# Loading w1 in nine 128-partition pieces, and a LayerNorm copy moved to VectorE

## The chip, the cores and the metric

The kernel runs on one core of a Trainium2 chip. The metric is the device time of one execution in microseconds. TensorE (PE) multiplies, VectorE (DVE), ScalarE (ACT) and GpSimd (POOL) do the elementwise work, and SyncE (SP) issues most of the transfers (DMAs), which run on 16 DMA engines shared by all issuing queues.

## The reference

A pre-LayerNorm block on `x` of 1 x 2048 x 576 in bf16: a linear attention mixer with 32 heads of 18, and then an MLP with 4608 hidden units. Both are added to their input.

```python
qkv = layernorm(x) @ wqkv                       # q, k, v: 32 heads x 18
phi(t) = concat(softmax(t @ w_phi[h]), softmax(-t @ w_phi[h]))   # 36 features a head
kv = phi(k)^T v;  z = sum over rows of phi(k)
o = phi(q) kv / (phi(q) z + 1e-6)
h = x + o @ wo
y = layernorm(layernorm(h))
out = h + gelu(y @ w1 + b1) @ w2 + b2           # w1: 576 x 4608, w2: 4608 x 576
```

## The kernel before

The 2048 rows are 16 tiles of 128, taken as 8 pairs. The code writes the order of every engine's work by hand (a manual schedule): each call below puts its instructions at the end of its engine's queue, and the semaphores are set by the tile framework. What stands earlier in the code runs earlier on that engine.

First comes everything that all rows are needed for: LayerNorm, transposes, the projection of keys and values, the softmax features, and the sums `kv` in a PSUM accumulator (`sums`, L586). The query features come in between. `table` turns the sums into the matrix `kvm`. Then `combine_mm` (L673) multiplies the first pair's transposed query features (`turn_q(0)`, two DMA transposes issued by SP at L572, from the tile `padded`) with `kvm`; `divide`, a transpose (`turn_o_mm`), `residual_mm` with `wo` (L722), the second LayerNorm (`residual_stats`, `second`, `rescale`) and its transpose (`turn2_mm`, L359) follow. `turn2_ev` (L364) copies that transpose from PSUM into `ln2T`, in two parts: five chunks and four chunks of the 576 columns, 64 columns of each tile's two halves a chunk.

Then the MLP. `up` (L1161) multiplies with w1, ScalarE applies GELU (L1183), `down` (L1205) multiplies with w2. The first block has 256 rows. Other pairs' attention work is put in between the products: `leave(1)`, at the third product of the first `down`, calls `combine_mm` for the second pair, whose query tile `turn_q(1)` transposes.

w1 lies in SBUF in two parts, `w1[0]` and `w1[1]`, each `[128, 9, 1152]`: partitions 0 to 63 hold 64 rows of each of nine chunks `c` for one range of 1152 hidden columns, partitions 64 to 127 the same rows for the range 2304 columns further on. `up` walks 18 pairs of 128-column blocks: pairs 0 to 8 read `w1[0]`, pairs 9 to 17 `w1[1]`, and each pair goes over all nine chunks. The DRAM view is

```python
w1v = B_w1.rearrange("(c k) (two f) -> two k c f", k=64, two=2)
```

`load_w1(q, ...)` (L613) issues a piece. The memory of `w1[0]` is lent to other weights until the query weights are folded. The first part's pieces are issued by SP at places in the hand-written order between L1002 and L1095, around the loads of `wo` (L624), `turn_q(0)` and `load_b2` (L638). `close_keys` frees the key tiles, makes `w1[1]` and the first half of w2 in their place, and issues the second part's pieces, by SP and GpSimd in turn. Behind them SP issues `load_w2` (L619) six times for the first half and twice for the second, then `turn_q(1)`, and the last four of w2.

Of the kernel before, what the change touches and what calls it, by code (L numbers as in the profile page):

```python
# [18 lines left out]
FF = 4608  # L19
# [10 lines left out]
KC = 9  # L30
KH = 64
# [14 lines left out]
def kernel(  # L46
# [13 lines left out]
    nc = tc.nc  # L60
# [62 lines left out]
    w1 = [w1_pool.tile([P, KC, FF // 4], BF16, name="w1_0", tag="w1_0")]  # L123
# [215 lines left out]
    pool, vec, syn, sca = nc.gpsimd, nc.vector, nc.sync, nc.scalar  # L339
# [6 lines left out]
    act, dve, gps = nc.scalar.copy, nc.vector.tensor_copy, nc.gpsimd.tensor_copy  # L346
# [16 lines left out]
    def turned_back(key, dst, part, copy):  # L363
        copy(dst[:, 5 * part : 5 + 4 * part, :], flight[key][part])  # L364
# [118 lines left out]
    def key_exp(p, i):  # L483
        if p not in phik:
            phik[p] = exk_pool.tile([P, 2, PW], BF16, name="phik", tag="exk")
        exponentials("k", phik[p], p, i)

    def query_mm(p, i):
        features("q", wqp, p, i, CROSSED)

    def query_exp(p, i):
        if p not in phiq:
            phiq[p] = take(("phiq", p)).rearrange("p (a f) -> p a f", a=2)
        exponentials("q", phiq[p], p, i)
# [23 lines left out]
    def key_weigh(p, i, a, eng):  # L518
        weigh("k", phik[p], p, i, a, eng)
# [10 lines left out]
    def query_weigh(p, part, a, eng):  # L530
        src = phiq[p][:, a, :].rearrange("p (h f) -> p h f", f=DH)
        rk = rescaled[p][:, a, :]
        n = 2 * WH
        g0 = part * 5
        hs = slice(g0 * n, (g0 + 5) * n)
        eng.tensor_tensor(  # L536
            padded[:, a, g0 * P : (g0 + 5) * P].rearrange("p (g k) -> p g k", k=P)[
                :, :, 0:STEP
            ].rearrange("p g (h f) -> p g h f", f=DH),
            src[:, hs, :].rearrange("p (g h) f -> p g h f", h=n),  # L540
            rk[:, hs].rearrange("p (g h o) -> p g h o", h=n, o=1).to_broadcast([P, 5, n, DH]),
            ALU.mult,
        )
        if part:
            m = 2 * COUNT[-1]
            eng.tensor_tensor(
                padded[:, a, KW * P - m * DH : KW * P].rearrange("p (h f) -> p h f", f=DH),
                src[:, 2 * NH - m :, :],
                rk[:, 2 * NH - m :].rearrange("p (h o) -> p h o", o=1).to_broadcast([P, m, DH]),
                ALU.mult,  # L550
            )
# [26 lines left out]
    def sums(p, a):  # L578
        t = 2 * p + a
        left.remove(t)  # L580
        for w in range(KW):
            n = COUNT[w]
            f0 = min(w * STEP, PW - P)
            b = w // 6
            at = (w - BANKS[b][0]) * WV
            nc.tensor.matmul(  # L586
                acc_kv[:, b, at : at + n * VW],
                phik[p][:, a, f0 : f0 + P],
                vals[:, t, FIRST[w] : FIRST[w] + n, :].rearrange("p h v -> p (h v)"),
                start=False, stop=not left, skip_group_check=True,  # L590
            )
# [15 lines left out]
    w1v = B_w1.rearrange("(c k) (two f) -> two k c f", k=KH, two=2)  # L607
    w2v = B_w2.rearrange("(h m p) f -> h p m f", h=2, p=P)
    w2 = []

    def load_w1(q, n, eng):
        c0, half = n // 2 * 3, n % 2
        eng.dma_start(  # L613
            w1[q][half * KH : (half + 1) * KH, c0 : c0 + 3, :],
            w1v[half, :, c0 : c0 + 3, q * FF // 4 : (q + 1) * FF // 4],
        )

    def load_w2(h, n):
        nc.sync.dma_start(w2[h][:, 3 * n : 3 * n + 3, :], w2v[h, :, 3 * n : 3 * n + 3, :])  # L619
# [22 lines left out]
    def close_keys():  # L642
        kctx.close()
        late = ctx.enter_context(
            tc.tile_pool(name="late", bufs=1, side="left", reuse_waits="tile")
        )
        w1.append(late.tile([P, KC, FF // 4], BF16, name="w1_1", tag="w1_1"))
        w2.append(late.tile([P, NM // 2, D], BF16, name="w2_0", tag="w2_0"))
        for n in range(6):
            load_w1(1, n, (nc.sync, nc.gpsimd)[n % 2])  # L650

    def side_pool(name, bufs):
        return ctx.enter_context(
# [56 lines left out]
    def turn_o_ev(part, copy):  # L710
        turned_back("o", oT[0], part, copy)
# [5 lines left out]
    def residual_mm(p, i, pa):  # L717
        cs = slice(i * HALF, (i + 1) * HALF)
        for c in range(KC):
            for a in range(2):  # L720
                rows = slice(a * KH, (a + 1) * KH)
                nc.tensor.matmul(  # L722
                    pa[a], oT[p % 2][rows, c, :], wo[rows, c, cs],
                    start=(c == 0), stop=(c == KC - 1),
                )
        flight["a", p, i] = pa
# [30 lines left out]
    def rescale(t, half):  # L757
        mv, rs = moved[t]
        normalise(ln2[t % 2][:, :, half, :], chunks(t), mv, rs, 0)
# [4 lines left out]
    def place2(t):  # L764
        return ln2T[:, :, t % 4 * P : (t % 4 + 1) * P]
# [7 lines left out]
    def turn2_ev(t, part, copy):  # L773
        turned_back(("2", t), place2(t), part, copy)

    def double_bank():
        pa = two.tile([P, 2, 512], FP32, name="pa", tag="two")
        return [pa[:, a, 0:HALF] for a in range(2)]

    def gelu_table():  # L780
        nc.scalar.activation(spare[:, :], mhalf[:, :], AF.Gelu_apprx_tanh)
# [217 lines left out]
    sums(2, 1)  # L999
    key_weigh(3, 1, 1, pool)  # L1000
    key_weigh(4, 1, 1, pool)
    load_w1(0, 4, syn)  # L1002
    sums(2, 0)
    key_weigh(4, 0, 0, pool)
    query_mm(5, 0)
# [15 lines left out]
    query_sum(0, 1)  # L1021
    key_exp(6, 0)
    key_exp(7, 0)
    load_w1(0, 1, syn)
    query_mm(4, 1)
    key_mm(6, 1)
    query_exp(4, 1)
    load_w1(0, 5, syn)
    query_weigh(0, 1, 0, pool)
    query_mm(6, 1)  # L1030
    key_sum(6, 0)
    key_sum(7, 0)
    key_weigh(7, 1, 0, pool)
    load_w1(0, 2, syn)
    key_exp(6, 1)
    value_mm(6, 0)
    query_exp(6, 1)
# [50 lines left out]
    query_mm(3, 1)  # L1088
    turn_o_mm()
    turn_o_ev(0, dve)  # L1090
    load_w1(0, 3, syn)
    query_mm(2, 0)
    turn_o_ev(1, dve)
    query_exp(2, 1)
    load_w1(0, 0, syn)  # L1095
    residual_mm(0, 1, double_bank())
    query_exp(3, 1)
    load_b2()
# [10 lines left out]
    query_mm(1, 1)  # L1109
    query_mm(5, 1)  # L1110
    close_keys()
    query_exp(1, 1)
    query_exp(5, 1)
# [8 lines left out]
    turn2_mm(0)  # L1122
    rescale(1, 0)
    rescale(1, 1)
    turn2_ev(0, 1, act)
    turn2_ev(0, 0, dve)
    gelu_table()
    load_w2(0, 0)
    load_w2(0, 1)
# [191 lines left out]
```

## Time and profile before

| what | us |
|---|---|
| median of 3 runs | 389.98 |
| lowest, highest run | 388.52, 390.71 |
| span of the profiled execution | 391.7 |
| TensorE busy in it | 383.0 |
| ScalarE, VectorE, GpSimd busy | 163.2, 166.0, 117.8 |

The runs shown were timed apart from the profiled execution, for which the page gives the span, 391.7 us from the first to the last instruction; nothing of it lies outside that. The profile names a group by line, engine, operation and tiles (`out<-in`); DRAM and SBUF tiles of w1 and w2 both show as `w`, w_phi's as well. `SPq` and `POOLq` are the queues in which SP and GpSimd issue transfers. "issue" in the chain is time in which the engine waited for nothing that the profile shows.

### The profile page before, as it was taken

The page shows a single profiled execution, that of the slowest core. Times are in us where ns is not written, and L with a number is a line of the kernel's source. Part 1 is how long each engine was busy: PE and PEld are TensorE (multiplying, and loading weights), DVE is VectorE, ACT ScalarE, POOL GpSimd, SP SyncE. Part 2 cuts the span into 40 slices and gives each one's busy share as a digit, 9 for nine tenths or more (in the row PEclk, how much of TensorE's full clock was granted, in tenths as well). Part 3 has the DMA queues.
Part 4 walks back from the last instruction along what each step waited for, and adds up shares of the span by engine and source line. Part 5 has one row for each costly group of instructions (what it writes and reads, how often), then busy time and mean ns, then how long its engine had stood idle before and what let it go on. Part 6 is the DMA issues. An engine that isn't in the chain of part 4 may idle for free.

```text
span 391.7 us, 10190 instructions
## 1 busy us (share of the span) xinstructions
PE 383.0 (98%) x4475; PEld 269.0 (69%) x4475; DVE 166.0 (42%) x364; ACT 163.2 (42%) x291; POOL 117.8 (30%) x161
## 2 busy tenths in 40 slices
PE   7999999799999999999999999999999999999997
PEld 3778779479978887844457887444677764447773
DVE  6998997385249388590019322000480000000100
ACT  2998995478500850046650000666300016661000
POOL 6399998116404654144003111000031110000120
PEclk9999999899999999999999999999999999999999
DMA  8977599999455578433003462000071000000000
GB/s 250 259 128 128 93 218 188 238 313 248 148 105 102 98 105 136 94 66 68 2 2 62 89 108 48 17 1 2 2 105 47 17 15 2 2 2 0 17 28 19
DMA packets 74096, 34.93 MB, mean 89 GB/s; under 512 B 61028, under 2 KB 71524, under 8 KB 74052
## 3 DMA queue, kind: packets, MB, share of 16 engines
q1 hardware_dynamic: 72944, 32.78, 40.3%
q0 software_dynamic: 336, 1.33, 1.2%
q8 instruction: 35, 0.57, 0.7%
q10 hardware_dynamic: 772, 0.17, 0.2%
q14 instruction: 9, 0.07, 0.1%
HBM read 16.47 MB, written 2.36 MB: 48 GB/s over the span
## 4 chain that ended last, share of the span: by engine, by line
PE 93%; ACT 2%; DMA 2%; issue 1%; DVE 1%; SPq 0%
PE po L1205 36%; PE ph L1161 36%; PE pk L450 8%; PE pv L450 5%; PE pa L722 4%; DMA w<-in_A_wqkv_dram 2%; PE acc_kv L586 1%; PE pn L673 1%; ACT home L472 1%; ACT shared L412 0%; DVE xh L731 0%; PE pW L419 0%; PE pW L405 0%; PE pT L359 0%; PE pX L377 0%
## 5 line engine op out<-in xcount | busy, mean ns | idle before, releaser
L1183 ACT ACTIVATE home<-ph,b1col 128x512 bf16<-128x512 f32 (+1 forms) x180 | 98.4, 598 | 169.1 <-PE ph L1161 165.9
L1205 PE MATMUL po<-w,home 128*128 128x288 bf16 (+2 forms) x1152 | 143.3, 286 | 0.0
L1161 PE MATMUL ph<-shared,w 64*128 64x512 bf16 (+2 forms) x1638 | 141.3, 331 | 0.6 <-ACT shared L364 0.6
L1205 PEld LDWEIGHTS <-home 128*128 128x128 bf16 x1152 | 109.4, 98 | 32.1 <-issue 1.8
L1161 PEld LDWEIGHTS <-w 64*128 64x128 bf16 x1638 | 80.3, 94 | 60.5 <-issue 0.7
L1209 DVE TENSOR_TENSOR ot<-po,hb 128x288 bf16<-128x288 f32 (+2 forms) x32 | 14.4, 453 | 106.4 <-PE po L1205 96.7
L450 PEld LDWEIGHTS <-home 64*128 64x128 bf16 x864 | 42.9, 95 | 13.6 <-issue 3.3
L1194 POOL TENSOR_TENSOR hb<-xh,b2bc 128x576 f32<-128x576 bf16 x16 | 20.4, 1273 | 104.6 <-DVE ot L1209 102.8
L536 POOL TENSOR_TENSOR padded<-home,rq 128x540 bf16<-128x540 bf16 x32 | 34.9, 1102 | 34.5 <-DVE rq L528 18.9
L731 DVE TENSOR_TENSOR xh<-pa,xh 128x288 bf16<-128x288 f32 x32 | 13.0, 447 | 72.4 <-PE pa L722 72.4
L274 POOL TENSOR_TENSOR rs<-va,mhalf 128x1 f32<-128x1 f32 x16 | 8.8, 549 | 110.9 <-DVE va L272 110.9
L507 POOL TENSOR_TENSOR phik<-phik,rk 128x576 bf16<-128x576 bf16 x28 | 33.4, 1218 | 1.4 <-DVE rk L503 1.2
L472 ACT ACTIVATE home<-pk 128x576 bf16<-128x576 f32 x32 | 18.6, 665 | 12.7 <-PE pk L450 10.4
L450 PE MATMUL pk<-wqp,home 64*128 64x288 bf16 x288 | 20.5, 293 | 2.8 <-issue 2.8
L501 DVE TENSOR_REDUCE sk<-phik 128x64 f32<-128x1152 bf16 x16 | 21.0, 1312 | 1.7 <-ACT phik L472 1.6
L527 DVE TENSOR_REDUCE sk<-home 128x64 f32<-128x1152 bf16 x16 | 21.0, 1310 | 0.0
L686 DVE RECIPROCAL rec<-pn 128x18 f32<-128x18 f32 (+1 forms) x32 | 8.0, 249 | 28.5 <-PE pn L673 28.5
L450 PE MATMUL pv<-wv,home 64*128 64x288 bf16 x288 | 19.6, 283 | 0.0
L472 ACT ACTIVATE phik<-pk 128x576 bf16<-128x576 f32 x32 | 18.7, 656 | 1.8 <-PE pk L450 1.1
L450 PE MATMUL pk<-shared,home 64*128 64x288 bf16 x288 | 19.3, 283 | 0.0
L722 PE MATMUL pa<-wo,shared 64*128 64x288 bf16 x288 | 18.6, 283 | 0.0
L722 PEld LDWEIGHTS <-shared 64*128 64x128 bf16 x288 | 13.9, 94 | 4.5 <-issue 0.5
(76 smaller groups left out, 208.3 us busy)
## 6 DMA issues: line engine op xcount, KB each, us to landing
w<-in_B_w_dram SPq DMA_DIRECT2D x21, 432.0 KB, 8.7
out_dram<-ot SPq DMA_DIRECT2D x15, 144.0 KB, 2.2
xh<-in_A_x_dram SPq DMA_DIRECT2D x3, 576.0 KB, 6.8
wo<-in_A_wo_dram SPq DMA_DIRECT2D x4, 324.0 KB, 8.0
w<-in_B_w_dram POOLq DMA_DIRECT2D x3, 432.0 KB, 13.0
wv<-in_A_wqkv_dram SPq DMA_DIRECT2D x2, 576.0 KB, 8.7
w<-in_A_wqkv_dram SPq DMA_DIRECT2D x1, 576.0 KB, 6.0
wqp<-wqp SPq DMA_DIRECT2D x2, 288.0 KB, 3.9
```

The costliest lines, as they stand in the source:

```text
L450: nc.tensor.matmul(dst[:, a, 0:HALF], lhs[rows, c, :], w[rows, slot, i * HALF : (i + 1) * HALF], start=(n == 0), stop=(n == KC - 1),)
L472: nc.scalar.activation(rows[:, :, i * HH : (i + 1) * HH, s, :], flight[key, p, i][:, :, 0:HALF].rearrange("p a (h f) -> p a h f", f=DH), A ...
L501: nc.vector.tensor_reduce(sk[:, :, :], part_of(dst, i), AX.X, ALU.add)
L507: eng.tensor_tensor(part, part, flight["r" + key, p, i][:, a, :].rearrange("p (h o) -> p h o", o=1).to_broadcast([P, NH, DH]), ALU.mult,)
L527: nc.vector.tensor_reduce(sk[:, :, :], part_of(phiq[p], i), AX.X, ALU.add)
L536: eng.tensor_tensor(padded[:, a, g0 * P : (g0 + 5) * P].rearrange("p (g k) -> p g k", k=P)[:, :, 0:STEP].rearrange("p g (h f) -> p g h f", ...
L722: nc.tensor.matmul(pa[a], oT[p % 2][rows, c, :], wo[rows, c, cs], start=(c == 0), stop=(c == KC - 1),)
L1161: nc.tensor.matmul(ph[half][:, lo:hi], w1[p_ // 9][rows, c, p_ % 9 * P : (p_ % 9 + 1) * P], ln2T[rows, c, base + lo : base + hi], start=(c ...
L1183: nc.scalar.activation(hidden(m), ph[half][:, 0:width], AF.Gelu_apprx_tanh, bias=b1col[:, m : m + 1], scale=1.0,)
L1194: nc.gpsimd.tensor_tensor(hb[:, :], xh[:, t, :], b2bc[:, :], ALU.add)
L1205: nc.tensor.matmul(po[:, :], hidden(m)[:, i_ * P : (i_ + 1) * P], w2[m // 18][:, m % 18, cs], start=(j == 0), stop=(j == NM - 1),)
L1209: nc.vector.tensor_tensor(ot[:, cs], po[:, :], hb[:, cs], ALU.add)
```

## The change

Each part of w1 is loaded in nine pieces, one for each chunk `c`, with 128 partitions and 1152 columns (288 KB), where it was six pieces of three chunks on 64 partitions (432 KB). The SBUF side of a piece is `[128, 1152]`, the DRAM side `[2, 64, 1152]`. The first part's nine loads take the six places of the order, in rising `c`; the bytes issued ahead of `wo` and `turn_q(0)` stay the same (four pieces of 432 KB before, six of 288 KB after). Of the second part SP issues five pieces and GpSimd four, where it was three each. The second copy of the first tile's transpose, `turn2_ev(0, 1, ...)`, moves from ScalarE to VectorE, behind the first copy.

```diff
-    def load_w1(q, n, eng):
-        c0, half = n // 2 * 3, n % 2
+    def load_w1(q, c, eng):
         eng.dma_start(
-            w1[q][half * KH : (half + 1) * KH, c0 : c0 + 3, :],
-            w1v[half, :, c0 : c0 + 3, q * FF // 4 : (q + 1) * FF // 4],
+            w1[q][:, c, :],
+            w1v[:, :, c, q * FF // 4 : (q + 1) * FF // 4],
         )
...
-        for n in range(6):
-            load_w1(1, n, (nc.sync, nc.gpsimd)[n % 2])
+        for c in range(KC):
+            load_w1(1, c, (nc.sync, nc.gpsimd)[c % 2])
...
-    load_w1(0, 4, syn)
+    load_w1(0, 0, syn)
+    load_w1(0, 1, syn)
...
-    load_w1(0, 1, syn)
+    load_w1(0, 2, syn)
...
-    load_w1(0, 5, syn)
+    load_w1(0, 3, syn)
+    load_w1(0, 4, syn)
...
-    load_w1(0, 2, syn)
+    load_w1(0, 5, syn)
...
-    load_w1(0, 3, syn)
+    load_w1(0, 6, syn)
+    load_w1(0, 7, syn)
...
-    load_w1(0, 0, syn)
+    load_w1(0, 8, syn)
...
-    turn2_ev(0, 1, act)
     turn2_ev(0, 0, dve)
+    turn2_ev(0, 1, dve)
     gelu_table()
```

## The prediction

> **What bounds the kernel now.** I read the page first (the chain, the queues and the list of DMA issues), then the chain in order of time, then the DMA queue's own timeline, then windows over the stage in which w1 is loaded.
>
> ```profile
> span 391.7 us, 10190 instructions
> PE 93%; ACT 2%; DMA 2%; issue 1%; DVE 1%; SPq 0%
> q10 hardware_dynamic: 772, 0.17, 0.2%
> xh<-in_A_x_dram ACTq DMA_DIRECT2D x1, 144.0 KB
> w<-in_A_w_phi_dram ACTq DMA_DIRECT2D x2, 9.0 KB, 3.5
> w<-in_A_w_phi_dram ACTq DMA_DIRECT2D x1, 2.5 KB
> out_dram<-ot SPq DMA_DIRECT2D x1, 16.0 KB, 1.4
> ```
>
> TensorE carries 93% of the chain: what delays it is paid in full, and it has no slack later to win anything back. So the question is which of its waits the change shortens or makes. From the chain in order of time (start, duration, what):
>
> ```profile
> 68.17 0.73 PE pn L673 x22
> 68.90 1.70 PE pk L450 x26
> 70.60 2.77 issue
> 73.37 0.86 PE pk L450 x10
> 85.48 0.48 ACT shared L364
> 86.00 17.88 PE ph L1161 x342
> 103.89 0.35 PE po L1205 x2
> 104.24 0.62 PE pn L673 x22
> 104.86 7.85 PE po L1205 x64
> ```
>
> At 68.17 TensorE multiplies with the first transposed query tile (L673), at 86.00 the MLP begins, at 104.24 the second query tile is needed. Two holes stand ahead of the MLP: 2.77 us at 70.60, which no instruction explains, and the ScalarE copy at 85.48. No step of the chain waits for w1. How the transfers stand in SP's queue, and w1's share of GpSimd's:
>
> ```profile
> 46.53 2.63 SPq L613 DMA_DIRECT2D w<-in_B_w_dram  x4
> 49.20 1.26 SPq L624 DMA_DIRECT2D wo<-in_A_wo_dram  x2
> 55.84 6.72 SPq L572 DMA_TRANSPOSE shared<-padded  x2
> 62.61 0.84 SPq L624 DMA_DIRECT2D wo<-in_A_wo_dram  x1
> 63.51 1.30 SPq L613 DMA_DIRECT2D w<-in_B_w_dram  x2
> 64.85 0.61 SPq L638 DMA_DIRECT2D b2bc<-in_B_b_dram  x1
> 67.03 1.93 SPq L613 DMA_DIRECT2D w<-in_B_w_dram  x3
> 69.08 16.87 SPq L619 DMA_DIRECT2D w<-in_B_w_dram  x8
> 91.78 3.13 SPq L572 DMA_TRANSPOSE phit<-padded  x2
> 94.97 4.85 SPq L619 DMA_DIRECT2D w<-in_B_w_dram  x4
> 67.65 2.08 POOL L613 DMA_DIRECT2D w<-in_B_w_dram  x3 [1.63 <-PE acc_kv L586]
> ```
>
> Four of the six pieces of w1's first part go out at 46.53, ahead of wo and of the transposes that the step at 68.17 reads. The reader should keep this order: the changed pieces stand in the same places. The next fence has busy time by engine in stretches (the last three columns are the TensorE clock, the DMA engines' busy share, GB/s), and one row of the DMA issues between 46 and 100 us:
>
> ```profile
> 6.00:9.00 3.00, 2.08 (x29) 1.53 (x26) 2.33 (x9) 0.87 (x1) 2.57 (x8) 1.00 1.03 378
> 50.00:56.00 6.00, 6.00 (x102) 4.78 (x98) 5.30 (x7) 5.52 (x12) 5.59 (x7) 1.00 1.07 215
> 67.00:73.40 6.40, 3.63 (x68) 2.60 (x67) 3.63 (x12) 2.39 (x4) 2.07 (x3) 1.00 1.06 212
> 73.40:77.00 3.60, 3.60 (x35) 2.42 (x37) 0.82 (x2) 1.19 (x2) 0.00 (x0) 0.58 1.05 250
> 86.00:90.00 4.00, 4.00 (x92) 4.00 (x93) 3.93 (x6) 3.85 (x8) 1.74 (x2) 1.00 1.07 355
> wo<-in_A_wo_dram SPq DMA_DIRECT2D x3, 324.0 KB, 11.4
> ```
>
> With 64-partition pieces in flight (50 to 56, 67 to 73.4) all 16 engines are busy, yet move 212 to 215 GB/s; with 128-partition loads (6 to 9, 86 to 90) they move 355 to 378. A wo load of 324 KB takes 11.4 us to land: 0.33 MB at 215 GB/s is 1.5 us, so it waited behind the w1 pieces issued before it (four of 0.44 MB, 1.77 MB, 8.2 us). Transfers of SP's queue are served in the order of issue.
>
> The Trainium skill ("SBUF — State Buffer", section "Door 1: The DMA port swizzle") says that DMA bandwidth depends on how many of SBUF's 16 ports the partitions reach, and that 64 partitions in a row reach 8. The trace agrees: 212 against 355. By that rule the change helps.
>
> **The change, part by part.**
>
> *How a new piece is split over the engines.* This decides the case, and the trace has no piece of the new shape. What it has is the ACT queue, with a query up to 3.43 us, when its first load is over:
>
> ```profile
> q10 hardware_dynamic: 144, 0.15, 14.2%
> ```
>
> The first load has 128 rows and shows 144 packets: 128 and one closing packet from each of 16 engines. The page has 772 in all, so 628 belong to the three w_phi loads, of 128x2, 128x2 and 72 rows of 36 bytes (9.0, 9.0 and 2.5 KB): 584 rows and 44 closing packets, which is 16 + 16 + 12. Seventy-two rows went to 12 engines, the largest number up to 16 that divides 72; dealt out as evenly as can be, 15 would have shared them. A transfer is thus cut into equal parts along its outermost dimension. The old piece has 64 rows outermost on both sides, so 16 engines. The new piece has 128 partitions outermost in SBUF, but the DRAM side is `w1v[:, :, c, ...]`, whose outermost dimension is the 2 of `two`, with 64 rows inside; the two steps (half a row, a whole row) cannot be merged into one of 128. Equal parts of both sides: 2 engines. The ends are 2 and 16; I take 2, since the nearest row (72 on 12) shows division and not filling up. Both ends are priced below.
>
> The Trainium skill ("DMA: Bandwidth & Descriptors", section "Why a DMA increments its semaphore by 16 and not by 1") states this: the number of engines is the largest up to 16 that divides the slowest dimension of both patterns. By that rule it is two, and on SP's queue always the same two; the row of 72 agrees, and no run here shows a slowest dimension of 2.
>
> *Price of a piece.* An engine at full rate moves 378 / 16 = 23.6 GB/s (6 to 9 us). Two take 0.295 MB in 6.24 us. The slow end is 212 / 16 = 13.3 GB/s, 11.1 us; I take 6.24, because the two parts write to the two halves of the partitions and nothing shares a port with them. So w1's first part costs 9 x 6.24 = 56 us on these two engines. In the second part SP issues 5 pieces (31 us); GpSimd's 4 go through its own queue, and I take them on other engines (a rival otherwise).
>
> *The queue of the two engines, step by step.* SP issues at 46.53; the first data flows 1.4 us later (my estimate from the page's 1.4 us for the shortest transfer), 47.9.
> - Six pieces (c = 0 to 5, all now ahead of wo): 37.4, to 85.3.
> - Two wo loads, each 0.33 MB / 378 GB/s = 0.9: to 87.1. The two transposes of the first query tile, 3.1 by their issue row at 91.78: to 90.2, landed (1.4) at 91.6. L673, at 68.17 before, starts 23.4 later; TensorE is in order, so all behind it waits, and with it ScalarE (the remaining exponentials) and VectorE (the divisions and LayerNorm), which have nothing else to do there.
> - From L673 to the MLP were 17.8 us. The hole of 2.77 falls in a pause and goes, and the copy's 0.5 (below): the MLP could begin at 91.6 + 14.5 = 106.1. But the third wo load (0.9) and pieces 6 to 8 (18.7) end at 109.8, landed 111.2. The first products need all nine chunks: start 111.2.
> - Nine of the 18 pairs of columns use the first part: 17.88 / 2 = 8.9, to 120.1. The tenth needs the second part: b2 (0.4) and five pieces (31.2) end at 141.4, landed 142.8: a wait of 22.7. The other nine pairs end at 151.7, or 153.2 with the clock at 0.58 for 3.6 us (row 73.40:77.00) after the pause, 1.5.
> - Behind these stand eight loads of w2 (0.44 MB / 378 = 1.17 each, 9.4) to 150.8 and the two transposes of the second query tile (3.1) to 153.9, landed 155.3. L673's second use, at 104.24 before, starts 51.1 later. The last four w2 loads (4.7) land at 160.0; the first down product uses the last of them 4.2 after L673's start (0.62 for L673, then 29 products of 7.85 / 64 = 0.123), at 159.5: 0.5 more.
>
> Sum: 51.1 + 0.5 = 52 us (rounded). Nothing after 104 depends on these engines in a new way, so it is neither won back nor grows.
>
> *More issues.*
>
> ```profile
> L613 SPq DMA_DIRECT2D w<-in_B_w_dram x9: 602/619/646, 46.5 to 68.3; - x9
> ```
>
> Each piece costs SP 0.62 us. Three more in the first part: two ahead of the wo loads, covered by SP's wait for `padded` until 55.84; without that cover 1.2 us. One more after it and two more in the second part, 1.9, go ahead of w2, whose place is set by the two engines. GpSimd issues one more, 0.62, idle until 82.07 (its next work is the second LayerNorm's). Costed at nothing, between 0 and 1.9.
>
> *The copy.*
>
> ```profile
> 84.61 0.48 DVE L364 COPY shared<-pT 128x640 bf16<-128x640 bf16 x1
> 85.33 0.62 ACT L364 COPY shared<-pT 128x512 bf16<-128x512 bf16 x1
> PE ph L1161 <- ACT shared L364: 0.6, 1, 0.6
> ```
>
> The ScalarE copy waits for the last exponential and holds TensorE 0.6. On VectorE it follows the first copy at 85.09 and takes 0.4 (four chunks against five in 0.48): ready at 85.5 against 85.95, a gain of 0.5. VectorE's next two copies wait for TensorE until 85.46, so they lose nothing; ScalarE reaches its table load sooner. Here it is hidden behind the wait for w1.
>
> Forecast: 390 + 52 = 442 us. The sum is made in an execution whose span is 391.7, 1.7 above the median 389.98; I add the difference to the median.
>
> **Rivals.**
>
> *The pieces use all 16 engines (the other side).* For it: the 128 partitions on the SBUF side, and 355 GB/s where loads fill them. Against: the 12 engines of the 72 rows. Then w1's 5.3 MB take 15 us instead of 25 and land earlier, but nothing on the chain waits for them; only the copy's 0.5 is left: 389.5. If the hole at 70.60 (2.77, and 1.5 of slow clock behind it) came from the crowded engines and goes, 385. It decides from about five engines on: six pieces, 1.77 MB, must be through between 47.9 and about 63 for the transposes to land by 68, 117 GB/s, five times 23.6.
>
> *GpSimd's pieces fall on the same two engines.* Nothing in the trace excludes it. Each that does adds 6.2 to the queue ahead of the second part's end: 448 for one, 467 for all four.
>
> *The two engines run at the contended rate.* 14 pieces x 4.9 more = 68 us: 510. Against: no neighbour on their ports.
>
> *The transposes are not held up.* If they go past the w1 pieces, L673 is on time, but the second part still lands at about 140; the sum stays within 4 us of the forecast. So no case of its own.
>
> **How the numbers follow.** Two engines 0.86: alone 0.52 (442), with one GpSimd piece 0.24 (448), all four 0.05 (467), at the contended rate 0.03, something milder between 395 and 426 0.02. Sixteen engines 0.14: 389.5 0.08, 385 0.06. About 0.5% (2 us) is what a measurement can tell from no change. One row of the DMA share by slices, from 3 to 9 us in 40 slices, gives the lower bound:
>
> ```profile
> GB/s 399 446 392 415 372 390 211 110 199 254 128 95 179 170 230 300 284 323 284 330 369 384 392 438 346 438 376 338 330 330 422 392 361 369 369 369 461 369 338 369
> ```
>
> Its fastest slice, 461, is 28.8 GB/s an engine, 5.1 us a piece, 14 x 1.1 = 16 less. Range: from there, 426, up to 460 (one GpSimd piece, and pieces at 355 GB/s / 16, 14 x 0.4, and further slow-clock stretches of 1.5 each); the first two cases lie in it, 0.76, and part of the third.
>
> **What will show it.** Few engines: a DMA busy share near 2/16 and under 60 GB/s from about 55 to 85; w1 issues with a landing of tens of us; L673 waiting for the transposes about 20 us; L1161 waiting for w1 at its tenth pair, about 20 us; the remaining stages as long as before. Sixteen engines would show 350 GB/s at 50 and 67 us, and L1161 at about 85.5. The forecast is wrong if w1's landings stay under 15 us.

## The result, and the profile after

| | before | after |
|---|---|---|
| median, us | 389.56 (388.52 to 390.71) | 453.26 (453.1 to 453.87) |
| span of the profiled execution, us | 391.7 | 451.3 |
| mean granted TensorE clock in it | 0.995 | 0.932 |

The change makes the kernel slower by a factor of 1.163 (95% interval 1.160 to 1.166), 63.7 us. Forecast were 442 us and a range of 426 to 460. The lines of the page that answer to those of before (the chain by engine, the first product with w1, the product with the first query tile, and GpSimd's own DMA queue, q0):

```profile
span 451.3 us, 10197 instructions
PE 75%; SPq 13%; DMA 8%; ACT 1%; DVE 1%; issue 1%; POOL 0%
L1163 PE MATMUL ph<-shared,w 64*128 64x512 bf16 (+2 forms) x1638 | 148.0, 342 | 22.3 <-DMA w<-in_B_w_dram 22.3
L672 PE MATMUL pn<-kvm,shared 128*128 128x57 bf16 (+1 forms) x22 | 1.2, 229 | 31.0 <-DMA shared<-padded 31.0
q0 software_dynamic: 2112, 1.19, 1.0%
```

TensorE's share of the chain fell from 93% to 75%. What took its place is SP's queue, an engine that computes nothing, and transfers. Two waits of TensorE make 53.3 us: 31.0 before it may use the first transposed query tile, 22.3 for w1. (Line numbers moved by one or two: L672 was L673, L1163 was L1161, L1207 was L1205.) SP's queue shows how it came about:

```profile
45.58 24.32 SPq L612 DMA_DIRECT2D w<-in_B_w_dram  x6
69.94 14.55 SPq L623 DMA_DIRECT2D wo<-in_A_wo_dram  x2
84.61 11.54 SPq L572 DMA_TRANSPOSE shared<-padded  x2
96.20 0.58 SPq L623 DMA_DIRECT2D wo<-in_A_wo_dram  x1
96.84 6.07 SPq L612 DMA_DIRECT2D w<-in_B_w_dram  x3
102.96 3.57 SPq L637 DMA_DIRECT2D b2bc<-in_B_b_dram  x1
106.72 26.02 SPq L612 DMA_DIRECT2D w<-in_B_w_dram  x5
132.85 18.82 SPq L618 DMA_DIRECT2D w<-in_B_w_dram  x8
152.19 7.20 SPq L572 DMA_TRANSPOSE phit<-padded  x2
```

Before, four issues of w1 took 2.63 us; now six take 24.32. Single issues take up to 6.83 us, where they took 0.62: SP cannot even hand over a piece before an earlier one has moved, and everything behind it in the order waits: the wo loads are issued at 69.94 instead of 49.20, the transposes at 84.61 instead of 55.84. The windows say why (the last two columns are the DMA engines' busy share and GB/s), and so does the count of packets from 50 to 56 us:

```profile
6.00:9.00 3.00, 2.65 (x37) 2.06 (x34) 2.90 (x10) 1.21 (x2) 2.58 (x7) 1.00 1.05 394
48.00:66.00 18.00, 18.00 (x353) 14.80 (x350) 15.18 (x17) 13.64 (x25) 16.62 (x15) 1.00 0.14 51
DMA packets 136, 0.31 MB, mean 51 GB/s; under 512 B 2, under 2 KB 2, under 8 KB 136
```

For 18 us the 16 engines are busy 0.14 of the time, about 2 of 16, and move 51 GB/s, 25.5 for each of two; at full load one moves 394 / 16 = 24.6. In 6 us about one piece passes, and it shows two short closing packets, where the load of 128 rows in the prediction, on 16 engines, shows 16. The other engines stand idle, and the queue still crawls.

### The profile page after: what moved, and what is told of

The parts are those of the page before. It is cut to its first block, busy times and chain, and to the rows that moved or that the text cites. A ratio compares the mean times of both kernels' runs of the same rounds, so it can differ in the third digit from the quotient of the medians.

```text
span 451.3 us, 10197 instructions
## 1 busy us (share of the span) xinstructions
PE 390.7 (87%) x4474; PEld 269.6 (60%) x4475; DVE 166.2 (37%) x365; ACT 162.8 (36%) x290; POOL 119.3 (26%) x162
## 4 chain that ended last, share of the span: by engine, by line
PE 75%; SPq 13%; DMA 8%; ACT 1%; DVE 1%; issue 1%; POOL 0%
PE po L1207 31%; PE ph L1163 27%; PE pk L450 7%; DMA w<-in_B_w_dram 6%; SPq L612 5%; PE pv L450 4%; PE pa L721 4%; SPq L572 3%; SPq L623 3%; DMA shared<-padded 1%; PE pn L672 1%; SPq L618 1%; PE acc_kv L586 0%; ACT shared L412 0%; DVE xh L730 0%
## 5 line engine op out<-in xcount | busy, mean ns | idle before, releaser
L1163 PE MATMUL ph<-shared,w 64*128 64x512 bf16 (+2 forms) x1638 | 148.0, 342 | 22.3 <-DMA w<-in_B_w_dram 22.3
L1207 PE MATMUL po<-w,home 128*128 128x288 bf16 (+2 forms) x1151 | 143.6, 286 | 0.5 <-DMA w<-in_B_w_dram 0.5
L1163 PEld LDWEIGHTS <-w 64*128 64x128 bf16 x1638 | 81.4, 98 | 87.8 <-DMA w<-in_B_w_dram 24.0
L1207 PEld LDWEIGHTS <-home 128*128 128x128 bf16 x1152 | 109.3, 98 | 32.9 <-issue 2.5
L672 PE MATMUL pn<-kvm,shared 128*128 128x57 bf16 (+1 forms) x22 | 1.2, 229 | 31.0 <-DMA shared<-padded 31.0
L672 PEld LDWEIGHTS <-shared 128*128 128x128 bf16 x22 | 1.1, 125 | 31.3 <-DMA shared<-padded 31.3
```

The source lines that it names most:

```text
L1163: nc.tensor.matmul(ph[half][:, lo:hi], w1[p_ // 9][rows, c, p_ % 9 * P : (p_ % 9 + 1) * P], ln2T[rows, c, base + lo : base + hi], start=(c ...
L1207: nc.tensor.matmul(po[:, :], hidden(m)[:, i_ * P : (i_ + 1) * P], w2[m // 18][:, m % 18, cs], start=(j == 0), stop=(j == NM - 1),)
```

## The experiments

Each ratio is to the kernel before.

**1. The copy alone.**

```diff
-    turn2_ev(0, 1, act)
     turn2_ev(0, 0, dve)
+    turn2_ev(0, 1, dve)
```

> Before with one edit: the second copy of the first tile's transpose goes to VectorE, w1 loaded as before. If the copy's step is right (ready 0.5 us sooner, nothing else late), the time is 0.3 to 0.6 us under before. Rival: TensorE's hole at the start of the MLP is w1's (the profile of before also names a w transfer there), and the time is unchanged within 0.2 us.

Measured: ratio 0.9996 (0.9981 to 1.0011). In the trace the step does what was said; the timeline of all engines at the start of the MLP has no wait ahead of the first product:

```profile
81.46 0.98 PE L359 MATMUL pT<-ident,shared 128*128 128x128 bf16 x13
82.51 0.28 PE L1161 MATMUL ph<-shared,w 64*128 64x128 bf16 x3
```

The 0.6 us wait for ScalarE's copy is gone, and nothing took its place. In the time it is not resolved: 0.5 us is 0.13%, inside the interval. So the copy has no part in the 64 us, and its gain is seen in the trace alone.

**2. All 16 engines, everything else as changed.**

```diff
-    w1v = B_w1.rearrange("(c k) (two f) -> two k c f", k=KH, two=2)
+    w1v = B_w1.rearrange("(c k) (two f) -> (k two) c f", k=KH, two=2)
...
-            w1v[:, :, c, q * FF // 4 : (q + 1) * FF // 4],
+            w1v[:, c, q * FF // 4 : (q + 1) * FF // 4],
```

> The changed kernel with one edit: w1's rows are read in another order, so that the DRAM side of a piece is one run of 128 rows with an even step of half a row, instead of 2 times 64. Sizes, number, order and queues of the pieces are the same; the values in w1 are permuted, so the output is not the reference's. Theory (two engines, because the DRAM side begins with a 2): 16 engines take part, 350 GB/s while w1 loads, L672 at about 68 us, time 389 (0.5 under before, or 385 if the 2.77 us hole goes for good). Rival (the smaller pieces, their number, or their order in front of wo cost the time): it stays above 440.

Measured: 388.92 us, ratio 0.9963 (0.9950 to 0.9976). Size, number, order and queue of the pieces are those of the changed kernel; one dimension on the DRAM side makes 64 us. Windows:

```profile
50.00:52.00 2.00, 2.00 (x38) 1.59 (x34) 1.83 (x3) 1.52 (x4) 2.00 (x3) 1.00 0.96 370
67.00:73.40 6.40, 5.89 (x106) 4.43 (x103) 3.91 (x13) 3.80 (x7) 2.39 (x4) 1.00 1.02 339
```

370 and 339 GB/s where before moved 215 and 212: full 128-partition pieces do load faster. The time falls by only 1.4 us, the copy's gain in it, since the kernel before waits for w1 nowhere. This trace has no hole at 70 us.

**3. The same pieces as two halves.** To keep w1's contents, each piece is issued as two of 64 partitions, with 64 rows outermost on both sides.

```diff
-        eng.dma_start(
-            w1[q][:, c, :],
-            w1v[:, :, c, q * FF // 4 : (q + 1) * FF // 4],
-        )
+        for two in range(2):
+            eng.dma_start(
+                w1[q][two * KH : (two + 1) * KH, c, :],
+                w1v[two, :, c, q * FF // 4 : (q + 1) * FF // 4],
+            )
```

> The changed kernel with each of its pieces issued as two, one for the 64 partitions of each half, so that both sides of a transfer have 64 rows outermost: eighteen issues a part, each of 147 KB; order, bytes and contents as in the changed kernel. Theory (a transfer's engines follow from its outermost dimensions): all 16 engines, L672 at 68 to 69; SP needs 0.62 us for each of nine more issues a part, which delays w2 by about 3 us: 389 to 393. Rival (small pieces in this order cost the time): above 420.

Measured: 389.99 us, ratio 0.9996 (0.9970 to 1.0022). Twice as many and smaller pieces, in the changed order, cost nothing. SP's queue:

```profile
45.93 8.07 SPq L613 DMA_DIRECT2D w<-in_B_w_dram  x12
55.45 6.52 SPq L572 DMA_TRANSPOSE shared<-padded  x2
79.47 6.21 SPq L619 DMA_DIRECT2D w<-in_B_w_dram  x8
```

Twelve issues take 8.07 us, 0.67 each, and the transposes go out on time. w2 goes out 10 us later than before, and nothing waits for it. Neither number, size nor order was the cause.

**4 and 5. Eight and four engines.** w1's DRAM side gets the shape 8 times 16 or 4 times 32 rows, in pieces of the same size; the edit shown is the one for four.

```diff
-    w1v = B_w1.rearrange("(c k) (two f) -> two k c f", k=KH, two=2)
+    w1v = B_w1.rearrange("(c k) (two f) -> c (k two) f", k=KH, two=2)
...
-            w1v[:, :, c, q * FF // 4 : (q + 1) * FF // 4],
+            w1v[0:4, c % 4 * 32 : (c % 4 + 1) * 32, q * FF // 4 : (q + 1) * FF // 4],
```

> The changed kernel with w1's DRAM side given the shape 8 times 16 rows (a step of 64 rows outside, half a row inside); same bytes and pieces, other values in w1. Theory (equal parts along the outermost dimension): 8 engines, a piece in 1.5 us, above the five engines from which I worked out that nothing waits: 389 to 391. Rival (any outermost dimension under 128 falls back to two or one engine): 440 or more.

> The same with 4 times 32 rows. Theory: 4 engines, a piece in 2.95 us; six pieces, wo and the transposes end at 70, landed 71 to 74 instead of before 68: L672 3 to 6 us late, the rest of w1 in time, the second query tile 3 to 6 us late: 393 to 398. Rival: as for 8 times 16, 440 or more; or no cost at all, 389.

Measured: 397.37 us, ratio 1.0170 (1.0142 to 1.0197) with 8; 421.92 us, 1.0791 (1.0765 to 1.0818) with 4. With the two of the changed kernel and the 16 of the second experiment the ladder is 453, 422, 397, 389. The mechanism holds (a window with four engines, from 50 to 55 us, is busy 0.27 and moves 101 GB/s: 25 an engine again), but both sizes were missed: 8 engines cost 6.7 us, not nothing, and 4 cost 31 instead of 3 to 8. "About five engines are enough" was wrong; with eight the wait lies at the second query tile, 4.3 us in two, and what holds its transposes there was not traced further. With four, L672 waited 23.4 us and the transposes stood in SP's queue for 21.47:

```profile
50.00:55.00 5.00, 5.00 (x86) 3.95 (x84) 4.90 (x6) 4.52 (x9) 4.58 (x6) 1.00 0.27 101
PE pn L672 <- DMA shared<-padded: 23.4, 1, 23.4
61.14 21.47 SPq L572 DMA_TRANSPOSE shared<-padded  x2
```

**6. Four engines without GpSimd's pieces.**

```diff
-            load_w1(1, c, (nc.sync, nc.gpsimd)[c % 2])
+            load_w1(1, c, nc.sync)
```

> The kernel with 4 times 32 rows, with all nine pieces of w1's second part issued by SP, none by GpSimd. That kernel came out at 422 where 393 to 398 was expected, and its transposes took from 67 to 88 us while GpSimd's pieces were moving. Theory (GpSimd's pieces share engines with SP's queue and take turns with it, packet by packet): without them L672 starts at 71 to 74 us instead of 90; the second part, 9 x 2.95 behind the first, lands at 108 and is waited for 11 us, the second query tile comes at 121: about 409. Rival (four engines are slow for transposes by themselves): L672 stays at 90 and the time goes to 422 + 12 = 434.

Measured: 420.7 us, ratio 1.0784 (1.0756 to 1.0811). The same two lines, and the wait for w1:

```profile
PE pn L672 <- DMA shared<-padded: 7.9, 1, 7.9
61.60 10.57 SPq L572 DMA_TRANSPOSE shared<-padded  x2
PE ph L1163 <- DMA w<-in_B_w_dram: 15.8, 5, 4.0
```

L672 waits 15.5 us less (23.4 and 7.9): GpSimd's pieces did hold up the transposes in the four-engine kernel. The whole stays the same because SP's queue has now nine pieces of the second part, and TensorE pays at L1163. My 409 was 12 us short: I had left three pieces of the first part, 3 x 2.95 = 8.9 us, out of the queue ahead of the second part, which was complete at 116.8 instead of 108. The other 3 us were not taken apart.

**7 and 8. Who issues the second part.** In the changed kernel, all nine pieces by GpSimd, or all nine by SP.

```diff
-            load_w1(1, c, (nc.sync, nc.gpsimd)[c % 2])
+            load_w1(1, c, nc.gpsimd)        # seven; nc.sync in eight
```

> The changed kernel with all nine pieces of w1's second part issued by GpSimd, none by SP. Theory (a GpSimd piece too runs on two engines, but on changing pairs): the second part lands by about 95, SP's two engines lose 29 us of work, the wait at the tenth pair is gone; the transposes are as late as in the changed kernel or 6 us later: 420 to 430. Rival (GpSimd's pieces stay on the same two engines as SP's): no better than the changed kernel, 453 or more.

> The changed kernel with all nine pieces of the second part issued by SP. Theory (in the changed kernel one of GpSimd's four pieces runs on SP's two engines while these are busy, and cost 6.4 us between 67 and 80): L672 starts at about 92 instead of 98, and the second part ends 4 x 5.75 - 6.4 = 17 us later: 470. Rival (no such meeting, the 6 us by which L672 came later than forecast have another cause): L672 stays at 98 and the time is 453 + 23 = 476.

Measured: 440.58 us, ratio 1.1280 (1.1252 to 1.1307) by GpSimd; 471.18 us, 1.2061 (1.2042 to 1.2081) by SP. The waits, GpSimd's kernel first, then SP's:

```profile
PE pn L672 <- DMA shared<-padded: 43.9, 1, 43.9
PE ph L1163 <- DMA w<-in_B_w_dram: 4.8, 1, 4.8
```

```profile
PE pn L672 <- DMA shared<-padded: 24.2, 1, 24.2
PE ph L1163 <- DMA w<-in_B_w_dram: 45.5, 9, 6.5
```

With none, four and nine of GpSimd's pieces L672 waits 24.2, 31.0 and 43.9 us. So the meeting of the two queues is shown: four pieces cost the changed kernel 6.8 us ahead of L672, the rival "one GpSimd piece falls on the same two engines" (6.2). The packets of the two queues show the sharing. The first two rows are the changed kernel from 72 to 76 us, the other two the seventh experiment from 74 to 82 (q0 is GpSimd's queue, q1 SP's; packets, MB, share of the 16 engines' time):

```profile
q0 software_dynamic: 171, 0.72, 47.3%
q1 hardware_dynamic: 28, 0.06, 4.2%
q0 software_dynamic: 928, 1.58, 87.4%
q1 hardware_dynamic: 49, 0.10, 9.5%
```

GpSimd's four pieces fill 0.473 x 16 = 7.6 engines, about two each, and SP's queue moves 7 packets a microsecond, where it moved 22 from 66 to 68: a third, so its two engines are among them. All nine by GpSimd removes the wait at the tenth pair, as expected, and fills 14 engines; but it holds up the transposes by 20 us instead of 7, so 440 and not 420 to 430. SP's queue is held to a third for about 10 us (72 to 82) instead of 5 (71 to 76), as if two of the nine pieces lay on its engines. That is not all of the 20, and the rest is open.

**9 and 10. One part in nine pieces, the other in six.**

```diff
-        for c in range(KC):
-            load_w1(1, c, (nc.sync, nc.gpsimd)[c % 2])
+        for n in range(6):
+            load_w1_six(1, n, (nc.sync, nc.gpsimd)[n % 2])    # nine; the first part in ten
```

> The changed kernel with only w1's second part loaded as before, in six pieces. Theory (one queue of two engines, in order): the transposes land at about 92, the first part at about 111; the second part comes soon behind, before its use at 120, so that wait is gone: 26 us over before, 416. Rival (each part costs by its bytes, half of the whole each): 421 here and the two halves add up to the whole 64.

> The changed kernel with only w1's first part loaded as before, in six pieces. Theory: five pieces at 5.8 us start behind 68 us and are through at 98 to 105, used first at 95; the w2 loads and the transposes of the second query tile behind them land at about 115 to 118 instead of 97: 10 to 14 us over before, 400 to 404. With the first part's 26 that is less than the whole 64, because the second part then waits in the queue behind the first. Rival (costs add): 38 us, 428.

Measured: 437.16 us, ratio 1.1204 (1.1172 to 1.1236) with the first part in nine; 413.04 us, 1.0584 (1.0556 to 1.0613) with the second. The excesses are 47 and 23, against forecasts of 26 and 10 to 14. They add to 70, not far above the 64 of both, so this pair does not tell a queue from costs that add: inconclusive on that point. What the traces do show is which wait each part makes: with the first part in nine, TensorE waits 31.7 us for the first query tile and 9.0 for w1; with the second, not at all for that tile and 17.3 for w1, as the steps of the prediction have it. The sizes were short in part because, of transfers that share the engines, I counted those of SP's queue only: in 6 us beside GpSimd's pieces SP's queue moves 34 packets in the ninth (74 to 80 us) and 44 in the tenth (75 to 81), where it moves 126 in 6 us once GpSimd's are through (the tenth, 84 to 90). How much of the missing 21 and 9 us that makes was not worked out.

**11. The first part behind the transposes.** The six early pieces are issued behind the wo loads and the transposes; the lines further up that lose them are left out here.

```diff
     load_wo(2)
+    for c in range(6):
+        load_w1(0, c, syn)
```

> The changed kernel with the first part's six early pieces issued behind the wo loads and the first query tile's transposes instead of ahead of them. Theory (the two engines' total work decides, not who is first): L672 is on time, 31 us of TensorE's longest wait gone, but w1's first part starts 16 us later and lands at 117 to 124, the second part at 146 to 153: 453 to 460, no gain. Rival (the late transposes are the cost): 453 - 31 = 422.

Measured: 462.56 us, ratio 1.1862 (1.1828 to 1.1895). TensorE's longest wait, 31 us, is gone, and the kernel is 9 us slower still, 2.6 us above the 453 to 460 that I expected:

```profile
63.13 48.50 SPq L612 DMA_DIRECT2D w<-in_B_w_dram  x9
PE ph L1159 <- DMA w<-in_B_w_dram: 62.1, 12, 6.1
```

(L1159 is L1163 of the changed kernel.) The same queue is paid at another place, and it started later. The longest wait was not the cost; the total work of two engines was.

**12. Both halves at once, with the contents right.** Before, with the copy on VectorE and the second part's pieces for partitions 64 to 127 issued by ScalarE beside SP's.

```diff
-        for n in range(6):
-            load_w1(1, n, (nc.sync, nc.gpsimd)[n % 2])
+        for n in range(1, 6, 2):
+            load_w1(1, n, nc.scalar)    # behind table(1); SP's three stay in place
```

> Before, with two edits: the copy on VectorE, and of w1's second part the three pieces of partitions 64 to 127 issued by ScalarE's queue at 67 us beside SP's three pieces of partitions 0 to 63 (GpSimd issues none), so that both halves are written at once. If the halves' ports are what held the load at 212 GB/s, the rate from 67 to 73 is 300 or more and the hole at 70 us closes: 388.5 to 389. Rival (the rate is set by something else in 64-partition pieces): 212 GB/s as before and 390.

Measured: 389.44 us, ratio 0.9983 (0.9962 to 1.0004), not told apart from before. In the stretch that I had named the rate did not rise, but later it did. The rows are two windows, and for the second of them the packets of SP's queue (q1) and ScalarE's (q10):

```profile
67.00:73.40 6.40, 6.07 (x105) 4.36 (x105) 4.45 (x14) 3.59 (x7) 0.00 (x0) 1.00 1.05 210
75.00:79.00 4.00, 4.00 (x70) 3.20 (x66) 3.56 (x13) 1.92 (x4) 0.79 (x2) 1.00 1.06 351
q1 hardware_dynamic: 323, 0.71, 52.9%
q10 hardware_dynamic: 327, 0.68, 51.2%
```

The 210 GB/s, like before's 212, are SP's queue alone: ScalarE issues from 67.19 us on, but its first packet of w1 moves just before 73. From 75 to 79 both queues carry 64-partition pieces of w1, one for each half, and move 351 GB/s, as much as the 128-partition pieces of the second experiment (339 to 370). So the 300 or more of the theory is reached, at a later time than I had named, and the rival's 212 is not what two queues give: two 64-partition transfers side by side do load at the rate of one of 128. Two queues that write the same half were not tried, so it is not shown whether the halves or the second queue raised the rate. The rule of the Trainium skill that I brought in for the 212 ("SBUF — State Buffer", section "Door 1: The DMA port swizzle": bandwidth by the number of ports reached) agrees with both, 212 for one half and 351 for two. Why the rate is still 221 GB/s from 73 to 75, with both queues moving, is open. The time stays because TensorE waits for w1 nowhere. There is no hole at 70 us in this execution, though the rate there was still 210, so it is not a higher rate that closed it.

## Why the prediction was right, and where its sum was short

The deciding step was right: a piece whose DRAM side begins with a dimension of 2 runs on two engines, read from 772 packets of another queue. The second and third experiments show it from both sides: change that dimension and the 64 us are gone. The Trainium skill ("DMA: Bandwidth & Descriptors", section "Why a DMA increments its semaphore by 16 and not by 1") is borne out for a slowest dimension of 2 by the two closing packets and the 51 GB/s. The steps:

| step | forecast | after |
|---|---|---|
| rate of the two engines, GB/s | 47.2 | 51 |
| L673, now L672, first use | 91.6 | 98.15 |
| w1's first part complete at TensorE | 111.2 | 118.4 |
| w1's second part complete | 142.8 | 149.7 |
| second query tile used (in the last column its second half) | 155.3 | 162.97 |

The rows of the last column are in the chain and in TensorE's timeline (the bracket has the wait ahead):

```profile
98.15 1.21 PE L672 MATMUL pn<-kvm,shared 128*128 128x57 bf16 x22 [30.98 <-DMA shared<-padded]
118.41 6.84 PE L1163 MATMUL ph<-shared,w 64*128 64x128 bf16 x80 [4.19 <-DMA w<-in_B_w_dram]
162.97 0.48 PE L672 MATMUL pn<-kvm,phit 128*128 128x57 bf16 x11 [1.88 <-DMA phit<-padded]
115.47 5.70 SPq L612
127.00 22.69 DMA w<-in_B_w_dram
```

- *GpSimd's pieces.* I had them on other engines in the likeliest case and kept the meeting as a rival at 0.24. It is what happened: all rows from L672 on are 6.5 to 7.7 us late, and without GpSimd's pieces L672 waits 6.8 us less and starts at 92.45, against the 91.6 of the forecast. The 448 for that rival is nearer than my 442; the eighth experiment, where the rival is absent, came out at 471.2 against a forecast of 470.
- *The hole.* I let the 2.77 us at 70.60 go as a gain, and the slow clock behind it cost nothing. That holds between the two profiled executions, but I added the result to the median, and the profiled execution of before is not a usual one: of 60 executions of before timed beside the experiments, 57 have spans of 387.0 to 389.9 at a clock of 0.999 to 1.0, three 391.0 to 391.6 at 0.996; the profiled one had 391.7 at 0.995. Between the two profiles lie 59.6 us, between the medians 63.7. The difference, 4.1, is about the size of the hole with the clock behind it (2.8 and 1.5). That it is the same time is not shown, since the timed executions have no trace, and the first experiment's trace, with w1 loaded as before, has a hole of 1.67 us at the same place, at full clock and with a span of 388.8. I knew that the span stood above the median, and did not ask whether what I took credit for was the reason.
- *The sum.* 51.6 (rounded to 52 there), and 7.6 for the second query tile, and 0.4 behind it, and 4.1 between profiles and medians, are 63.7.
- *Where TensorE waits.* I had 5.1 us for the first part (106.1 to 111.2) and one wait of 22.7 at the tenth pair. It waited 4.2 for the first part and then chunk by chunk, four waits and 18.1 us in all.
- *The point from which it decides* was far off: five engines, where the ladder has 6.7 us left at eight.
- *Other terms.* Each piece took 5.7 us (SP's issue in the last fence, which ends as the piece ahead makes room) against 6.24, which made up for part of the above. The extra issues cost nothing, as said: eighteen a part in the third experiment do not either. The copy's 0.5 us is seen in the trace and not in the time.

## What to carry to other kernels

Before a transfer is reshaped, look at the outermost dimension of both of its sides, and not at the partitions that it fills: in this kernel 2, 4, 8 and 16 engines gave 453, 422, 397 and 389 us for the same bytes. A DMA busy share of 2/16 with SP stuck in its issues is the mark of it in a profile, and the longest wait of the engine that computes may be any transfer behind in the queue. And where the profiled execution stands above the median of the timed ones, first ask which of its holes the others do not have.

## What the runs showed that was not expected

- Two queues that share engines hold each other up by more than their bytes. With four engines the pair of transposes stood in SP's queue for 21.47 us beside GpSimd's pieces and for 10.57 without them. The four pieces are 1.18 MB, 4.3 us for the 11 engines that they take when alone (69.3% of 16, from 82 to 84 us) at the 25 GB/s an engine measured above (an estimate), and the transposes lost 10.9.
- SP stops at the issue itself when few engines take a transfer: 24.32 us for six issues, against 2.63 for four, so that even transfers for idle engines are not handed over.
- Two queues that write both halves of the partitions at once moved 351 GB/s (the twelfth experiment, 75 to 79 us), where one queue with 64-partition pieces moved 210 to 215; 128-partition pieces reached 339 to 370. In the twelfth ScalarE's packets came 5 to 6 us behind their issue, and a window that ends soon after that hardly shows them.
